# A reordered opening for a Fourier mixing and channel mix kernel: x on 96 partitions with one stride, mu turned by TensorE, small work on GpSimd

The kernel runs on one core of one Trainium2 chip. The metric is the device time of one execution in microseconds (us). Several executions are timed, and medians are quoted. The span in a profile, from the first to the last instruction, is 1.7 to 1.9 us shorter than the device time of the same execution, so spans and times can be compared by that difference.

## The reference

```python
def _attn_ref(x):                       # x: 8 x 3072 x 256
    X = np.fft.fft(x, axis=1)
    X = np.fft.fft(X, axis=2)
    return X.real.astype(np.float32)

def _moe_ref(x, mu_k, mu_r, w_k, w_v, w_r):
    x_prev = np.concatenate([zeros, x[:, :-1, :]], axis=1)
    xk = mu_k * x + (1.0 - mu_k) * x_prev
    xr = mu_r * x + (1.0 - mu_r) * x_prev
    k = np.maximum(xk @ w_k, 0.0)       # 256 x 1024
    v = k * k @ w_v                     # 1024 x 256
    r = 1.0 / (1.0 + np.exp(-(xr @ w_r)))
    return (r * v).astype(np.float32)
# the result is _moe_ref(_attn_ref(x), ...)
```

## The kernel before

Each batch goes through five stages. Stage A sums x over 48 rows with cosine and sine weights `w_pm`. Stage D does the transform over the 256 features with `w_eo`. Stage C does the rest of the transform over the rows with `m1` and `m2`. VectorE then forms `y`, its difference `d` to the previous row, and the mixes `x = y + mu * d`. The products follow: k pieces, a square, v tiles, and an r item with a sigmoid. The second half of the rows (`m = 1`) is the mirror image of the first, and for it the mixes need mu with its feature blocks swapped (`mu_m`). TensorE runs matmuls on zeros (`keep_busy`) where it would stand idle in the opening. From about 40 us on, it works without rest on the products of one batch and the transforms of the next.

```python
    def load_part(b, h, n, q0, nq):              # two loads of 48 partitions
        for g in range(2):
            r0 = 32 * g + 16 * h + q0
            nc.gpsimd.dma_start(out=xh_t[b, h][48 * g:48 * g + 48, q0:q0 + nq],
                                in_=x_r[b, :, r0:r0 + nq, :])

    def keep_busy(n):
        ps = ps_v()
        for _ in range(n):
            nc.tensor.matmul(out=ps[:, 0:512], lhsT=zeros[:, 0:P], rhs=zeros, ...)

    def gather(dst, w, n):                       # rows of w in the order of row_i
        nc.gpsimd.indirect_dma_start(dst, None, w,
                 bass.IndirectOffsetOnAxis(ap=row_i[:, n:n + 1], axis=0))

    def loads():
        V.memset(mu_f, 0.0)
        # ... mu: six small loads on the SP queue ...
        for a in range(2):
            gather(wk_sb[0][a], moe_w_k, a)
        for i, mu in enumerate(mus):
            gather(mu_f[:, 1, i:i + 1], mu, 1)
        load_xh(1, 0)
        for a in range(2):
            gather(wr_sb[0][a], moe_w_r, a)
        nc.gpsimd.dma_start(out=wv_sb, in_=moe_w_v.rearrange("(fc p) v -> p fc v", p=128))
        load_xh(1, 1)
        for a in range(2):
            gather(wk_sb[1][a], moe_w_k, 2 + a)
        for a in range(2):
            gather(wr_sb[1][a], moe_w_r, 2 + a)

    # ... stages A, D, C of batch 0; then each step of the k loop runs k_piece,
    # the "x" items due at it, a v_tile, and the "w" items due at it ...
    at(5, plain_128)                             # small tables, on VectorE
    at(7, mirrored_mu)                           # mu_m, on VectorE
```

## Time and profile before

| kernel before | value | from |
|---|---|---|
| median of 3 timed runs | 457.84 us (457.7 to 458.09) | the times |
| the profiled execution | 461.26 us, span 459.5 us | the same list, one line below |
| TensorE busy | 447.2 us, 97% | the page |
| ScalarE, VectorE busy | 358.8, 360.0 us, 78% each | the page |
| TensorE busy from 10 to 20, 20 to 30, 30 to 40 us | 7.45, 6.66, 9.26 us | busy time by stretch |
| first v tile | 35.75 us | TensorE's timeline |

The profile is of one execution, and this one took 3.4 us longer than the median.

"Time lost" by a moment is that moment less the matmul work that TensorE has begun by then, with fillers left out and each matmul priced at its start-to-start distance in a packed run (512 columns 214.5 ns, 256 columns 108.7 ns, and so on). The useful work of the whole program is 434.2 us in either kernel, so time lost can be compared between kernels with different orders.

### The profile page before, as it was taken

What the parts mean: (1) busy time and instruction counts of PE and PEld (TensorE: products, weight loads), DVE (VectorE), ACT (ScalarE), POOL (GpSimd) and SP (SyncE); (2) the same over time, 40 slices, a digit from 0 to 9 for tenths busy, and PEclk for the clock granted to TensorE, in tenths of its full rate; (3) what the DMA queues carried; (4) which work ended last, traced back from release to release, by engine and by line L of the source; (5) the groups of instructions that cost most, each with busy time, mean ns of one, the idle gap of its engine ahead of it and who ended that gap; (6) DMA issues with size and microseconds to landing.
All of it is one profiled execution on the core that took longest, in us unless ns stands there. A gap on an engine that the chain in (4) does not pass through costs nothing.

```text
span 459.5 us, 9804 instructions
## 1 busy us (share of the span) xinstructions
PE 447.2 (97%) x4087; PEld 327.6 (71%) x4087; DVE 360.0 (78%) x532; ACT 358.8 (78%) x398; POOL 35.6 (8%) x67
## 2 busy tenths in 40 slices
PE   8879999999999999999999999999999999999996
PEld 4647777777777777777777777777777777676764
DVE  7779988987788877978698777888679855898453
ACT  4689898888877887888887888878887888666661
POOL 8831000000000000000000000000000000000000
PEclk9999999999999999999999999999999999999999
DMA  7894561626622274214722265212222221223223
GB/s 131 128 177 90 120 140 46 124 64 138 124 62 67 49 146 109 70 48 90 164 68 58 59 136 120 69 48 69 55 63 61 56 70 47 71 64 75 70 68 93
DMA packets 32972, 40.25 MB, mean 88 GB/s; under 512 B 4480, under 2 KB 30592, under 8 KB 31584
## 3 DMA queue, kind: packets, MB, share of 16 engines
q1 hardware_dynamic: 28080, 25.07, 21.9%
q0 software_dynamic: 4688, 14.42, 18.8%
q8 instruction: 32, 0.52, 0.5%
q10 hardware_dynamic: 160, 0.13, 0.1%
q14 instruction: 12, 0.10, 0.1%
HBM read 28.84 MB, written 25.17 MB: 118 GB/s over the span
## 4 chain that ended last, share of the span: by engine, by line
PE 93%; ACT 3%; DMA 1%; POOL 1%; issue 1%; DVE 0%; another core or an unknown queue 0%; POOLq 0%
PE psV L592 36%; PE psW L555 35%; PE psW L578 9%; PE psW L431 5%; PE psW L407 4%; PE psW L458 3%; DMA xh<-in_x_dram 1%; ACT rl L565 1%; ACT g_all L395 1%; PE psW L421 1%; POOL xh L106 1%; ACT a L395 0%; ACT L583 0%; ACT pq L395 0%; ACT m L287 0%
## 5 line engine op out<-in xcount | busy, mean ns | idle before, releaser
L565 ACT ACTIVATE rl<-psW 128x1024 f16<-128x1024 f32 x192 | 196.7, 1026 | 80.8 <-PE psW L555 80.4
L555 PE MATMUL psW<-x,wk 128*128 128x512 f16 (+1 forms) x776 | 197.4, 377 | 2.5 <-ACT rl L565 1.5
L592 PE MATMUL psV<-wv_sb,k 128*128 128x256 f16 x1536 | 198.6, 272 | 0.0
L571 DVE TENSOR_TENSOR k<-rl 128x2048 f16<-128x2048 f16 x96 | 117.4, 1224 | 62.5 <-ACT rl L565 61.8
L592 PEld LDWEIGHTS <-k 128*128 128x128 f16 x1536 | 143.7, 98 | 20.3
L555 PEld LDWEIGHTS <-wk 128*128 128x128 f16 x776 | 75.7, 98 | 53.3 <-issue 4.0
L602 DVE SCALAR_TENSOR_TENSOR o<-psV,r 128x512 f32<-128x512 f32 (+1 forms) x97 | 66.3, 684 | 22.9 <-PE psV L592 20.7
L523 DVE TENSOR_TENSOR x<-y,t 128x1536 f16<-128x1536 f16 (+1 forms) x70 | 61.8, 882 | 2.4
L395 ACT ACTIVATE a<-psW 128x768 f16<-128x768 f32 x62 | 49.6, 806 | 4.0 <-PE psW L421 2.1
L578 PE MATMUL psW<-wr,x 128*128 128x256 f16 x384 | 49.8, 273 | 0.0
L583 ACT ACTIVATE r<-psW 128x1024 f16<-128x1024 f32 x48 | 49.0, 1021 | 0.8 <-PE psW L578 0.8
L578 PEld LDWEIGHTS <-x 128*128 128x128 f16 x384 | 37.6, 98 | 14.4 <-issue 0.2
L395 ACT ACTIVATE g_all<-psW 128x1024 f16<-128x1024 f32 (+1 forms) x46 | 46.9, 1022 | 1.1 <-PE psW L431 1.1
L106 POOL DMA_DIRECT2D xh<-in_x_dram x38 | 19.7, 525 | 238.7 <-DVE eo L119 222.7
L431 PEld LDWEIGHTS <-a 128*128 128x128 f16 x384 | 25.1, 98 | 10.0 <-issue 0.2
L407 PEld LDWEIGHTS <-eo 96*128 96x128 f16 x416 | 23.4, 97 | 11.6
L119 DVE TENSOR_TENSOR eo<-xh 96x2048 f16<-96x2048 f16 x26 | 31.5, 1213 | 0.0
L395 ACT ACTIVATE pq<-psW 128x896 f16<-128x896 f32 (+5 forms) x33 | 28.7, 871 | 1.6 <-PE psW L431 1.1
L431 PE MATMUL psW<-w_eo,a 128*128 128x128 f16 x368 | 27.7, 219 | 0.0
L407 PE MATMUL psW<-w_pm,eo 96*128 96x96 f16 x416 | 26.3, 205 | 0.0
L458 PEld LDWEIGHTS <-g_all 128*128 128x128 f16 x459 | 17.8, 98 | 7.7 <-issue 0.7
L510 DVE TENSOR_SCALAR t<-d,mu_f 128x1536 f16<-128x1536 f16 (+1 forms) x38 | 20.6, 543 | 0.1
(106 smaller groups left out, 158.5 us busy)
## 6 DMA issues: line engine op xcount, KB each, us to landing
out_dram<-o SPq DMA_DIRECT2D x190, 128.0 KB
xh<-in_x_dram POOLq DMA_DIRECT2D x28, 384.0 KB
xh<-in_x_dram POOLq DMA_DIRECT2D x6, 192.0 KB
wv_sb<-in_moe_w_v_dram POOLq DMA_DIRECT2D x1, 512.0 KB
xh<-in_x_dram POOLq DMA_DIRECT2D x4, 96.0 KB
out_dram<-o ACTq DMA_DIRECT2D x2, 64.0 KB
out_dram<-o SPq DMA_DIRECT2D x2, 64.0 KB
y<-f SPq DMA_DIRECT2D x7, 3.4 KB
```

Source lines behind the costliest of these rows:

```text
L395: nc.scalar.activation(out=out_ap, in_=in_ap, func=AF.Copy)
L407: nc.tensor.matmul(out=ps[:, 128 * i:128 * i + 96], lhsT=eo[:, 8 * j + i, e, :], rhs=w_pm[0:96, 0], start=True, stop=True)
L431: nc.tensor.matmul(out=_v(ps, 256 * i + 64 * (1 - e), [(128, 2), (1, 64)]), lhsT=a_t[b][:, e, 2 * u:2 * u + 2, :], rhs=w_eo[:, e, :], star ...
L458: nc.tensor.matmul(out=ps[:, o + 64 * i:o + 64 * i + 64], lhsT=g_all[:, u, col:col + 128], rhs=m[:, sl] if sl != 1 else mz[:, 0 if m is m1 ...
L523: V.tensor_tensor(out=dst, in0=_v(y_t[b], 64 * (NSL * a + lo + 3 * m), [(1, n)]), in1=_v(x_t["t", a], 64 * lo, [(1, n)]), op=ALU.subtract ...
L555: nc.tensor.matmul(out=st["k", ds][:, 512 * hs + lo:512 * hs + hi], lhsT=wk_sb[m][a][:, 128 * fc:128 * fc + 128], rhs=xk[:, a, 512 * i + l ...
L565: nc.scalar.activation(out=st["rl"][:, 2 * ds:2 * ds + 2], in_=st["k", ds].rearrange("p (f t) -> p f t", f=2), func=AF.Relu, bias=0.0, sca ...
L571: V.tensor_tensor(out=k2_t[c][:, 2 * ds - 2:2 * ds + 2], in0=r, in1=r, op=ALU.mult)
L578: nc.tensor.matmul(out=ps[:, 256 * tb:256 * tb + 256], lhsT=x_t[b, 1, m][:, a, 512 * i + 128 * tb: 512 * i + 128 * tb + 128], rhs=wr_sb[m] ...
L583: nc.scalar.activation(out=st["r", c], in_=ps, func=AF.Sigmoid)
L592: nc.tensor.matmul(out=st["v"][:, 256 * h:256 * h + 256], lhsT=k2_t[c][:, fc, 128 * tb:128 * tb + 128], rhs=wv_sb[:, fc], start=(fc == 0), ...
L602: V.scalar_tensor_tensor(out=o.rearrange("p a b -> p (a b)")[:, 0:256 * n], in0=st["v"][:, 0:256 * n], scalar=16.0, in1=st["r", c][:, 256 ...
```

## The change

The intent: end the opening sooner. x comes with one load of 96 partitions per part, since the row index is now split so that one stride serves all of them. mu comes as two plain rows and is turned to columns by four small matmuls, so two gathers and six small loads go. GpSimd computes the feature angles, and later `m_last`, `plain_128` and the mirror of mu. Stage A's evacuations (the copies of its results out of PSUM, where matmuls write) alternate between ScalarE and VectorE. The first k pieces come ahead of the rest of the long sine, stage D and stage C. The fillers fall from 22 matmuls to 17.

```diff
-    def load_part(b, h, n, q0, nq):
-        for g in range(2):
-            r0 = 32 * g + 16 * h + q0
-            nc.gpsimd.dma_start(out=xh_t[b, h][48 * g:48 * g + 48, q0:q0 + nq],
-                                in_=x_r[b, :, r0:r0 + nq, :])
+    def load_part(b, h, q0, nq):
+        nc.gpsimd.dma_start(out=xh_t[b, h][:, q0:q0 + nq],
+                            in_=x_r[b, :, 16 * h + q0:16 * h + q0 + nq, :])
@@
-    keep_busy(11)
+    keep_busy(10)
@@
+    def mu_turn():
+        ps = ps_v()
+        for a in range(2):
+            for i in range(2):
+                c = 2 * a + i
+                nc.tensor.matmul(out=ps[:, c:c + 1], lhsT=mu_p[:, a, i], rhs=one, ...)
+        V.tensor_copy(out=mu_f.rearrange("p a i -> p (a i)"), in_=ps[:, 0:4])
@@
+    def m_last():
+        ts = nc.gpsimd.tensor_scalar
+        for out, src, by in ((m2[hi64, 25], m1[hi64, 25], -1.0), ...):      # four
+            ts(out=out, in0=src, scalar1=by, scalar2=None, op0=ALU.mult)
+        for m in (m1, m2):
+            nc.gpsimd.memset(m[lo64, 25], 0.0)
@@ loads
-        for i, mu in enumerate(mus):
-            gather(mu_f[:, 1, i:i + 1], mu, 1)
@@ plain_128: V.tensor_copy, V.memset, V.tensor_scalar become
+        ts = nc.gpsimd.tensor_scalar
+        # ... four of 64x26, four of 64x1, one of 128x1, three memsets ...
@@
     def mirrored_mu():
         for a in range(2):
-            V.tensor_copy(out=mu_m[:, a], in_=mu_f[:, 1 - a])
-        V.tensor_copy(out=mu_m[0:1], in_=mu_f[0:1])
+            nc.gpsimd.tensor_copy(out=mu_m[:, a], in_=mu_f[:, 1 - a])
+        nc.gpsimd.tensor_copy(out=mu_m[0:1], in_=mu_f[0:1])
@@ the order of the opening and of the first steps
-    keep_busy(3)
+    keep_busy(1)
+    a_sum(0, 0, 8, "V")
@@
-    keep_busy(2)
-    a_sum(0, 1, 0)
-    a_sum(0, 1, 4, "V")
+    a_sum(0, 1, 0, "V")
+    a_sum(0, 1, 4)
+    mu_turn()
@@
+    at(1, m_sine, NS1, NSL)
+    at(2, m_last)
+    at(3, d_pair, 0, 16)
+    at(5, plain_128)
+    at(5, mirrored_mu)
     (many more items moved; cut)
```

## The prediction

> **What bounds the kernel now.** I read the page first, then the busy time by stretch, then the engines' timelines of the first 40 us. The page's line of busy time and its row of PE slices:
>
> ```profile
> PE 447.2 (97%) x4087; PEld 327.6 (71%) x4087; DVE 360.0 (78%) x532; ACT 358.8 (78%) x398; POOL 35.6 (8%) x67
> ...
> PE   8879999999999999999999999999999999999996
> ```
>
> TensorE (PE) is the bound everywhere but in the first three slices (11.5 us each) and the last. The stretches say how far that goes (columns: window, its length, then busy us of PE, weight loads, DVE, ACT, POOL, then clock, DMA share, GB/s written):
>
> ```profile
> 0.00:10.00 10.00, 8.71 (x47) 4.98 (x48) 7.84 (x41) 4.25 (x6) 8.40 (x27) 1.00 0.76 123
> 10.00:20.00 10.00, 7.45 (x99) 5.87 (x98) 7.57 (x25) 5.85 (x10) 8.31 (x10) 1.00 0.78 118
> 20.00:30.00 10.00, 6.66 (x71) 4.49 (x70) 7.44 (x23) 8.18 (x10) 6.65 (x8) 1.00 1.13 178
> 30.00:40.00 10.00, 9.26 (x95) 6.65 (x93) 9.65 (x27) 9.97 (x12) 0.59 (x2) 1.00 0.47 84
> 40.00:50.00 10.00, 10.00 (x94) 7.23 (x92) 9.79 (x20) 8.49 (x11) 1.51 (x3) 1.00 0.94 174
> ...
> 200.00:400.00 200.00, 200.00 (x1858) 147.42 (x1856) 154.84 (x197) 163.47 (x180) 4.03 (x8) 1.00 0.33 75
> ```
>
> From 40 us to the tail PE never rests, and its matmuls run at their stream rate (eight of 256 columns in 0.87 us, four of 512 in 0.86). The change leaves that work alone, so it can only win before 40 us. Where PE stood or ran filler there:
>
> ```profile
> 1.18 4.87 PE L142 MATMUL psV<-zeros 128*128 128x512 f16 x11 [1.18 <-DVE zeros L136]
> ...
> 11.80 2.14 PE L421 MATMUL psW<-w_pm,xh 96*128 96x192 f16 x24 [1.29 <-DMA xh<-in_x_dram]
> ...
> 15.22 0.59 PE L142 MATMUL psV<-zeros 128*128 128x512 f16 x2 [0.62 <-ACT a L395]
> ...
> 25.31 1.02 PE L555 MATMUL psW<-x,wk 128*128 128x512 f16 x4 [0.92 <-ACT rl L565]
> 26.23 0.61 PE L431 MATMUL psW<-w_eo,a 128*128 128x128 f16 x8
> 28.37 0.82 PE L421 MATMUL psW<-w_pm,xh 96*128 96x192 f16 x8 [1.53 <-issue]
> ...
> 37.43 1.02 PE L555 MATMUL psW<-x,wk 128*128 128x512 f16 x4 [0.64 <-ACT r L583]
> ```
>
> The useful work that PE had done by 37.43, counted from the code and priced at start-to-start distances in this trace: stage A sums of batch 0, 64 matmuls x 82 ns = 5.3; stage D, 48 x 56 ns = 2.7; stage C, 75 x 29 ns = 2.2; six k pieces x 0.86 = 5.2; one r item 0.9; one v tile 0.9; three stage A sums of batch 1 x 0.66 = 2.0. Sum 19.2 us. So 37.4 - 19.2 = **18.2 us lost in the opening**. About 6 of them end with the first useful matmul at 5.85 (start, weights w_pm, first x) and stay. At most some 12 us (2.6%) are there to win, and 2% would need 9.2 of them.
>
> The waits are of two kinds. Until 16 us it is x: 11.66 us passed before its second half was there. From 18 to 38 us it is ScalarE (ACT), which evacuates nearly everything, with three PSUM slots behind it. It also stood still twice with work queued:
>
> ```profile
> 20.29 1.03 ACT L395 ACTIVATE g_all<-psW 128x1024 f16<-128x1024 f32 x1 [0.92 <-PE psW L431]
> ...
> 27.29 1.02 ACT L395 ACTIVATE pq<-psW 128x1024 f16<-128x1024 f32 x1 [1.11 <-PE psW L431]
> ```
>
> The second drains stage C matmuls that by their records ended at 24.4 us; PE's semaphore came at 27.27. With 0.41 before the activation at 28.73 that is 2.4 us which I cannot explain; later in the run I found no such lag. It matters below.
>
> **What the Trainium skill says.** (1) "DMA: Bandwidth & Descriptors", Rules for kernel authors: two transfers to disjoint partition halves gain nothing over one, as both spread over the same 16 engines; its Specifications put the HBM limit of a core near 358 GB/s. The trace agrees: from 6 to 11 us 172, 193, 168, 166, 191 GB/s of fp16 were written, mean 178, read as fp32 at twice that, 356. So one load of 96 partitions in place of two of 48 saves issue time on GpSimd, not bytes. (2) "ScalarE: Activation LUTs", What ACT_TABLE_LOAD costs: an activation takes 186 ns + 0.833 ns per column, and neighbours overlap by 93 ns; the trace agrees (1026 ns for 1024 columns, 1039 by the formula). (3) "TensorE: Matmul & The Clock Gate", Part 1: a cold array runs at half rate for about 3.4 us; the first 11 fillers took 443 ns each against 213 later. One filler fewer at the front shouldn't move that. (4) "SBUF — State Buffer", Who interferes with whom: some VectorE (DVE) modes lock GpSimd out of its port. The trace before neither shows nor excludes it (small GpSimd tensor_scalars took 190 to 400 ns); moving angles to GpSimd invites it.
>
> **The change part by part.**
>
> *x loads.* Each part was two issues of some 0.5 us (the first pair 1.24 to 2.41); it becomes one. Five parts save about 2.5 us of GpSimd. But the stream is at the HBM limit from 4 us on, so x arrives earlier only by the fuller start (61 and 119 GB/s in the third and fourth us): about 0.6 us, 11.0 for 11.66.
>
> *Feature angles on GpSimd.* Two 128x128 and one 128x1 tensor_scalar, estimate 0.4 + 2 x 0.5 us, between the second and third x load. GpSimd has that time from the line above; the third load is still issued by about 5.2, before the first two have drained. VectorE loses 0.15 + 0.48 of work there, off the path.
>
> *Zeros of g_all.* Of VectorE's 0.65 + 0.14 us, to ScalarE: 11 x 128 columns, an estimate of 1.36 us by (2), plus two of 0.2. With the table load until 2.0 and three copies of mu it ends near 4.7, where the sine of w_pm is due (4.8 now). No cost, if the mu rows (two plain loads) have landed by 4.
>
> *mu.* Six tiny loads, two GpSimd gathers (14.11 to 16.77) go. Four small matmuls come, estimate 0.7 us of PE in front of the last stage A items. The gathers delayed batch 1 and the other weights. GpSimd should now end its issues near 23 instead of 27.87, and the loads land by about 31 instead of 34.5. Nobody on PE waits for them in the trace before.
>
> *Stage A evacuations.* From seven on ScalarE (0.81 each, 0.48 the half) and two on VectorE to an alternation (0.96 on VectorE). After x at 11.0: items end on PE at 11.7, 12.3, then mu 13.0, 13.7, 14.0, 14.4; VectorE has mu's copy, m_ends (1.0), eo_rest (0.34), then the last half-size item, 14.5 to 15.05. Stage D starts at 15.1 for 15.81: **0.7 us won**.
>
> *Stages D, C.* d_half copies 0.60 (ACT) and 0.69 (DVE) as before; the first C item 16.6 (16.88 now); ScalarE drains C, C, D, D by 20.3; the nine-to-seventeen C item now comes before k: PE 20.35 to 21.05, then the k halves to 22.8.
>
> *The start of the k loop.* This is the large part. The long second sine (1.24) shrinks to 10 slices (about 0.85), and the rest of stage D, stage C, the r item and batch 1's sums are put behind the first four k pieces. ScalarE: relu k0, k1 by 24.3, sine 25.1, k2 26.1, k3 27.1 (32.29 now). One square (1.23) later, 28.4, the first v tile can run (35.75 now). From there at one ScalarE instruction of 1.0 us after another: d_halves, k, D, k, C, k, sigmoid table 1.28 and r 1.02 by about 36, then two sums of batch 1. PE follows: k4 by 25.4, D item 26.4, an idle stretch of about 2 us for the square, v 29.3, and on with small waits, the largest on r near 36, to the end of the fourth v tile at **39.0 us**. By then it has done 5.3 + 2.7 + 2.2 + eight k pieces 6.9 + four v tiles 3.5 + r 0.9 + four sums 2.6 = 24.1 us. Lost: 39.0 - 24.1 = **14.9 us against 18.2: 3.3 won**. mu's matmuls are counted among the lost.
>
> *The rest* (plain_128, m_last, mu's mirror on GpSimd): about 2 us of VectorE work after 35 us, where PE is the bound: nothing.
>
> My schedule has ScalarE never stalled unexplained. Of the 2.4 us of now I let a third return, 0.8. **3.3 - 0.8 = 2.5 us: 457.84 becomes 455.3 us**, 0.5%.
>
> **The rivals.**
> (a) *ScalarE is the wall and hardly gets lighter.* It was 99.7% busy from 30 to 40 us; the evacuations moved off it are about 1.6 us of some 25, while zeros and mu rows come only while it idles. If the late lags return in full, or VectorE's chain (96% there) sets the pace instead, the gain is 0.5 to 1: 457. For it: VectorE gets 1 us more work in 11 to 15 us. Against it: what moves behind is work that the later slack (78% busy) absorbs.
> (b) *x sets everything.* If x still lands at 11.66, stage D starts at 15.7 and 0.6 is lost: 456.
> (c) *The lags belong to GpSimd's gathers*, since they came among them and never later; fewer and earlier gathers would clear them. Then 3.3 and a little more, as the reordered start has no 1.5 us hole: 453.5 to 454.5.
> (d) *GpSimd or mu late*: angles held up by VectorE's port, or the mu copies in front of w_pm's sine waiting for a load; each us there delays x or the first matmuls one for one: up to 459.
>
> **Range and chances.** The centre is 455.3. (a) and (b) make 456 to 457, (c) 453.5; runs agree within 0.1%. Eight in ten: 452.8 to 457.3. Over 2% faster is below 448.7, which needs three quarters of all that can be won at all: 0.03. Over 2% slower is above 467, a mishap such as PE cold for many us: 0.02.
>
> **What would show it.** Right: first x issue near 0.6 us on GpSimd and x's second half at about 11; stage D near 15.1; first v tile near 28.5; PE without waits from about 39; the stretch from 40 us on as now; ScalarE near full from 20 to 38. Wrong: stage D not before 15.6 (b); ScalarE idle behind finished matmuls for 2 us or more (a); none at all (c); an early wait of ScalarE on mu (d). A change of PE's busy time after 60 us would refute the first step, that only the opening can move.

## The result

The changed kernel took **458.61 us** in the median (457.98 to 459.18, 4 runs), the kernel before 457.92 us in the same rounds (457.7 to 458.09). The ratio is 1.0015, 95% interval 0.9998 to 1.0032. A ratio here and below is the mean time of one kernel's fast runs over that of the other's of the same rounds, so not quite the ratio of the medians quoted. The time was outside the range of 452.8 to 457.3 us, and the gain of 2.5 us did not come.

The page of the changed kernel, the same two lines as in the prediction:

```profile
PE 446.3 (98%) x4090; PEld 327.8 (72%) x4090; DVE 356.9 (78%) x497; ACT 360.6 (79%) x407; POOL 35.6 (8%) x71
...
PE   8989899999999999999999999999999999999995
```

Its busy time by stretch, with the columns named in the prediction:

```profile
10.00:20.00 10.00, 8.96 (x131) 7.40 (x129) 8.72 (x26) 6.87 (x11) 8.51 (x14) 1.00 0.92 131
20.00:30.00 10.00, 8.87 (x88) 5.99 (x86) 8.06 (x13) 9.57 (x12) 3.94 (x4) 1.00 1.08 208
30.00:40.00 10.00, 9.55 (x83) 7.01 (x81) 9.21 (x13) 9.03 (x12) 6.08 (x12) 1.00 0.28 54
40.00:50.00 10.00, 8.78 (x87) 6.50 (x85) 8.06 (x13) 7.55 (x10) 3.92 (x12) 1.00 0.64 123
...
200.00:400.00 200.00, 200.00 (x1856) 147.52 (x1853) 156.03 (x199) 163.19 (x179) 2.03 (x4) 1.00 0.33 75
```

TensorE gained work from 10 to 40 us, as planned. But from 40 to 50 us, where it had been busy for 10.00 of 10 us, it now shows 8.78. TensorE's timeline has the milestones and the new hole:

```profile
9.74 1.49 PE L441 MATMUL psW<-w_pm,xh 96*128 96x192 f16 x16 [0.28 <-DMA xh<-in_x_dram]
...
14.62 0.61 PE L451 MATMUL psV<-w_eo,a 128*128 128x128 f16 x8
...
26.46 0.60 PE L615 MATMUL psV<-wv_sb,k 128*128 128x256 f16 x4 [0.80 <-ACT g_all L415]
...
47.63 0.81 PE L578 MATMUL psW<-x,wk 128*128 128x512 f16 x3 [1.22 <-DVE x L547]
```

The first line is x's second half (11.80 before), the second stage D, the third the first v tile. In the kernel before, stage D and the first v tile stood at

```profile
15.65 0.61 PE L431 MATMUL psV<-w_eo,a 128*128 128x128 f16 x8
...
35.75 1.04 PE L592 MATMUL psV<-wv_sb,k 128*128 128x256 f16 x8
```

The last line of the changed kernel is a k piece that waits for the mixed x of the second half of the rows. Who kept VectorE from mixing it stands in VectorE's timeline of the changed kernel:

```profile
43.31 0.62 DVE L534 TENSOR_SCALAR t<-d,mu_m 128x1536 f16<-128x1536 f16 x1 [1.84 <-POOL mu_m L678]
```

and why GpSimd was late, in GpSimd's:

```profile
33.45 2.93 POOL L351 TENSOR_SCALAR m<-m 64x64 f16<-64x64 f16 x4 [8.60 <-DMA wr<-in_moe_w_r_dram,row_i]
...
38.15 3.23 POOL L400 TENSOR_SCALAR tw<-m 64x26 f16<-64x26 f16 x4
...
41.60 1.07 POOL L404 TENSOR_SCALAR tw<-tw 64x1 f16<-64x1 f16 x4
...
43.10 0.18 POOL L678 COPY mu_m<-mu_f 1x4 f32<-1x4 f32 x1
```

GpSimd had issued its last gather by 24.86 us. Then it stood for 8.60 us until the last gathered weights had landed, although its next four instructions (`m_last`) read no weights, and what they do read was there when VectorE's `m_swap` ended at 25.87 us. The program's own wait list for the first of them holds the semaphores of the late gathers, which came at 31.3, 32.6, 32.9 and 33.3 us. Why the compiler put them there I did not find out. After `m_last`, twelve small instructions of `plain_128` lie in front of the mirror copy.

Time lost in the two profiles, and in one of the experiments below (the kernel before with its late loads held back):

| time lost by | 15 us | 20 | 25 | 30 | 40 | 45 | 50 | 60 | 400 | span |
|---|---|---|---|---|---|---|---|---|---|---|
| before, first profile | 9.8 | 12.2 | 14.3 | 17.1 | 18.2 | 18.4 | 18.5 | 18.5 | 20.3 | 459.5 |
| changed, first profile | 9.4 | 11.3 | 11.7 | 13.1 | 13.9 | 13.9 | 15.2 | 15.4 | 17.0 | 456.6 |
| before_gated | 9.8 | 12.0 | 13.0 | 13.8 | 15.2 | 15.4 | 15.4 | 15.6 | 17.3 | 456.5 |

Two things stand out. The profiles differ by 4.3 us at 40 us and by 2.9 us in span, yet the timed runs differ by nothing. And the changed kernel hands back 1.3 us between 45 and 50 us. The first is a question of which execution the profile caught. The second is a wait that the change created.

### The profile page after: what moved, and what is told of

Same layout as the page of the kernel before. It is cut to its first block, busy times and chain, and to the rows that moved or that the text cites. A ratio compares the mean times of both kernels' runs of the same rounds, so it can differ in the third digit from the quotient of the medians.

```text
span 456.6 us, 9765 instructions
## 1 busy us (share of the span) xinstructions
PE 446.3 (98%) x4090; PEld 327.8 (72%) x4090; DVE 356.9 (78%) x497; ACT 360.6 (79%) x407; POOL 35.6 (8%) x71
## 4 chain that ended last, share of the span: by engine, by line
PE 89%; POOL 5%; DMA 2%; DVE 2%; issue 1%; POOLq 0%
PE psV L615 35%; PE psW L578 34%; PE psW L601 9%; PE psW L451 4%; PE psW L427 4%; PE psW L482 2%; DMA wr<-in_moe_w_r_dram,row_i 2%; POOL wk L359 1%; POOL wr L359 1%; POOL tw L400 1%; POOL m L351 1%; DVE x L547 0%; POOL row L290 0%; DVE t L534 0%; POOL w_eo L395 0%
## 5 line engine op out<-in xcount | busy, mean ns | idle before, releaser
L547 DVE TENSOR_TENSOR x<-y,t 128x1536 f16<-128x1536 f16 x60 | 57.5, 959 | 2.1
L601 PEld LDWEIGHTS <-x 128*128 128x128 f16 x384 | 37.6, 98 | 14.6 <-DVE k L594 0.4
L415 ACT ACTIVATE pq<-psW 128x896 f16<-128x896 f32 (+5 forms) x33 | 28.5, 868 | 0.9 <-PE psW L482 0.9
L104 POOL DMA_DIRECT2D xh<-in_x_dram x19 | 10.2, 540 | 225.6 <-DVE eo L117 224.5
L482 PEld LDWEIGHTS <-g_all 128*128 128x128 f16 x459 | 17.8, 98 | 7.9 <-ACT g_all L415 1.1
L534 DVE TENSOR_SCALAR t<-d,mu_m 128x1536 f16<-128x1536 f16 x32 | 19.7, 615 | 1.8 <-POOL mu_m L678 1.8
```

Of the source, the lines that this page charges most:

```text
L415: nc.scalar.activation(out=out_ap, in_=in_ap, func=AF.Copy)
L547: V.tensor_tensor(out=dst, in0=_v(y_t[b], 64 * (NSL * a + lo + 3 * m), [(1, n)]), in1=_v(x_t["t", a], 64 * lo, [(1, n)]), op=ALU.subtract ...
L601: nc.tensor.matmul(out=ps[:, 256 * tb:256 * tb + 256], lhsT=x_t[b, 1, m][:, a, 512 * i + 128 * tb: 512 * i + 128 * tb + 128], rhs=wr_sb[m] ...
```

## The experiments

The questions were: is the profile of the kernel before typical of it; what does the wait for mu's mirror cost; and what are the late TensorE semaphores, seen as ScalarE standing idle behind matmuls that have long ended? A semaphore is the counter by which one engine tells another that a result is ready. "Late" below means that TensorE's semaphore came more than 0.12 us behind the end of its matmul. They were looked for on all engines, and only TensorE's were found late. But in the nine profiles that have late ones, 6 to 20 updates of the semaphores of TensorE, VectorE and ScalarE left no record at all, and in the other eleven at most one. So the others' may have been late unseen, and whether the recording itself takes part in the lateness was not tested. The kernels of one call ran on one chip and share the runs of the kernel before.

### First call: both kernels again, and GpSimd's small work back on VectorE

*before_again*: no edit, the kernel before.

> The kernel before, unchanged, profiled a second time. Theory P (untypical profile): the profiled execution from which I predicted took 461.26 us, 3.4 us more than the 457.84 of the unprofiled ones, and the excess is the three late PE semaphores in its opening; a second profile has a span near 456.1 us, no semaphore of PE more than 0.2 us behind its matmul, and only some 14.8 us lost in the opening. Rival R (the profile was right): the span is again near 459.5 us with the same lags at 18.7 to 21 and 24.4 to 28.8 us, so the opening has 18.2 us lost in every run. Ratio of the timed runs 1.000 under both.

Measured: 458.91 us against 459.69 (11 runs, 458.57 to 461.87) of the same kernel beside it, ratio 0.9977 (0.9942 to 1.0013). That two sets of runs of one kernel differ by 0.23% on one chip is the yardstick for all ratios below. The span was 457.4, and 16.2 us were lost by 40 us, not 18.2. There were late semaphores again, between 17.1 and 28.3 us, by up to 1.9 us instead of 2.9. So neither theory held as it stood: the kernel before need not lose 18.2 us, but its late semaphores were no single accident.

*after_again*: no edit, the changed kernel.

> The changed kernel, unchanged, timed in more rounds and profiled again. Both theories: ratio 1.000 to 1.003 as on record, span 456.2 to 457.4 us, TensorE waiting 1.2 us near 46.4 us for VectorE's mix, which waits for GpSimd's mirror of mu. If the profile of this kernel shows that wait in one execution only, it isn't the place where the gain went.

Measured: 459.92 us, ratio 0.9997 (0.9962 to 1.0032), with two slow runs of six (466.99 and 466.94 us at a mean clock of 0.98 and 0.985). The profile lost 16.4 us by 40 us. Here the changed kernel has late semaphores too (17.1 to 25.0 us), and with TensorE behind, the wait for the mirror costs only 0.2 us between 45 and 50.

*after_mu_v*: the mirror on VectorE.

```diff
         for a in range(2):
-            nc.gpsimd.tensor_copy(out=mu_m[:, a], in_=mu_f[:, 1 - a])
-        nc.gpsimd.tensor_copy(out=mu_m[0:1], in_=mu_f[0:1])
+            V.tensor_copy(out=mu_m[:, a], in_=mu_f[:, 1 - a])
+        V.tensor_copy(out=mu_m[0:1], in_=mu_f[0:1])
```

> The changed kernel with the mirror of mu (three tiny copies) back on VectorE; all else on GpSimd as changed. Theory G (GpSimd's chain of small operations gives back part of the opening's gain): TensorE's 1.2 us wait near 46 us goes, VectorE pays 0.4 us off the path, time 1.0 to 1.3 us less than the changed kernel, ratio to before 0.998 to 0.999. Rival (that wait is covered by later slack or by the next bound): same as the changed kernel within 0.3 us.

Measured: 461.27 us, ratio 1.0016 (0.9978 to 1.0053), two slow runs of six. The wait itself was gone (17.8 us lost at 45, 17.7 at 50), but the profile shows 17.6 lost by 40 us: late semaphores at 23.9 and 25.4 us, and a clock that was cut to half from 15.3 to 18.7 us. The run could not tell what the wait is worth. The mend was timed again in the fifth call.

*after_small_v*: `m_last`, `plain_128` and the mirror all on VectorE (`nc.gpsimd` becomes `V` in the three).

```diff
     def m_last():
-        ts = nc.gpsimd.tensor_scalar
+        ts = V.tensor_scalar
@@ plain_128
-        ts = nc.gpsimd.tensor_scalar
-        nc.gpsimd.memset(w_eo[:, 0, 63:64], 1.0)
+        ts = V.tensor_scalar
+        V.memset(w_eo[:, 0, 63:64], 1.0)
     (the other memsets and the mirror likewise)
```

> The changed kernel with all its small late GpSimd operations (last fixes of m, plain_128, mirror of mu) back on VectorE. Theory G: no better than moving the mirror alone, since only the mirror is on the path; VectorE has about 2.2 us more work near 26 and 37 us, where it is 92% busy, so 0 to 1 us slower than with the mirror alone moved: ratio to before 0.998 to 1.001. Rival (GpSimd's operations hold up VectorE's through the shared port as well): faster than the mirror alone by 0.5 us or more.

Measured: 461.87 us, ratio 1.0039 (1.0007 to 1.0071), one slow run of six. Late semaphores again, and a new loss of 1.4 us from 50 to 60 us, where VectorE is now behind. To move all of the small work back is too much.

### Second call: late loads held back, gathers removed, the mirror early

*before_gated*: in the kernel before, x's last part for batch 1 and the four late gathers wait for a relu of the k loop, by a one-element copy on GpSimd that reads its result.

```diff
-        load_xh(1, 1)
-        for a in range(2):
-            gather(wk_sb[1][a], moe_w_k, 2 + a)
-        for a in range(2):
-            gather(wr_sb[1][a], moe_w_r, 2 + a)
+    gate_t = const.tile([1, 2], FP16)
+    def late_loads(part):
+        nc.gpsimd.tensor_copy(out=gate_t[0:1, part:part + 1], in_=st["rl"][0:1, 0, 0:1])
+        if part == 0:
+            load_xh(1, 1)
+        else:
+            (the four gathers)
@@
+    at(0, late_loads, 0)
+    at(4, late_loads, 1)
```

> The kernel before, with batch 1's second x load held back until the first relu (25 us) and the second halves of w_k and w_r until the fifth (some 33 us), each by a one-element GpSimd copy that waits for it. What I want to know is why TensorE's semaphores come up to 2.9 us late in the opening of the profiles so far (at 16 to 21 and 20 to 29 us), and never later. Theory D (the saturated DMA queues delay them): with less in flight after 24 us the late ones at 24 to 29 us are gone or shrink below 0.5 us, and the fast runs gather at 456 to 457.5 us, 1 us or more below the kernel before. Rival I (the indirect loads and the small packets of w_v at 22 to 27 us): late ones as before, same time.

Measured: 458.29 us against 458.72, ratio 1.0004 (0.9982 to 1.0025); one run of the kernel before took 949.95 us and is left out. No late semaphore, 15.2 us lost by 40 us, span 456.5. ScalarE's timeline of before_again, in which an evacuation waits behind TensorE:

```profile
25.43 1.02 ACT L395 ACTIVATE pq<-psW 128x1024 f16<-128x1024 f32 x1 [0.98 <-PE psW L431]
```

and the same evacuation in before_gated, with no wait:

```profile
24.11 1.03 ACT L402 ACTIVATE pq<-psW 128x1024 f16<-128x1024 f32 x1
```

It is the instruction that waited 1.11 us and started at 27.29 in the first profile of the kernel before. Between these three executions of practically one instruction stream it starts at 24.11, 25.43 and 27.29.

*before_nogather*: plain strided loads in place of all gathers, and no row numbers computed for them on GpSimd (`rows()` goes). The rows come in a wrong order, so the result is wrong.

```diff
     def gather(dst, w, n):
-        nc.gpsimd.indirect_dma_start(dst, None, w,
-                                     bass.IndirectOffsetOnAxis(ap=row_i[:, n:n + 1], axis=0))
+        # row 0 or 128, then 64 and 63 rows with a step of 2
+        nc.gpsimd.dma_start(out=dst[0:1], in_=w[first:first + 1])
+        for p0, m, k in ((1, 64, 1), (65, 63, 2)):
+            ...
+            nc.gpsimd.dma_start(out=dst[p0:p0 + m], in_=src)
```

> The kernel before with each indirect load in place of which stand three plain strided loads of the same bytes; the upper halves come in ascending order, so the result is wrong on purpose. Theory D: late semaphores of TensorE as before, time the same within 1 us. Rival I (indirect loads): none late by more than 0.2 us, 1 to 3 us faster.

Measured: 458.68 us, ratio 1.0014 (0.9991 to 1.0038), no late semaphore, 14.9 us lost by 40 us. So the gathers cost nothing else that TensorE feels. But the next kernel shows that this chip had no late semaphores even with gathers, so the run does not settle who makes them.

*after_fix*: the mirror is copied by VectorE right behind mu's columns, and four fillers come back.

```diff
         V.tensor_copy(out=mu_f.rearrange("p a i -> p (a i)"), in_=ps[:, 0:4])
+        for a in range(2):
+            V.tensor_copy(out=mu_m[:, a], in_=mu_f[:, 1 - a])
+        V.tensor_copy(out=mu_m[0:1], in_=mu_f[0:1])
@@
-    keep_busy(1)
+    keep_busy(3)
@@
     mu_turn()
+    keep_busy(2)
@@
-    at(5, mirrored_mu)
```

> The changed kernel with the mirror of mu made by VectorE right after mu is turned (0.5 us at 12.5 us) and four more fillers (two before the third stage A item, two after mu is turned). Theory G with cold clock: the wait at 46 us is gone in every execution, and the fillers keep the array's clock from being cut between 9 and 19 us, so no run is slow (2 of 6 were, at clocks of 0.98) and the fast ones lie at 456.5 to 458.5 us, about 1 us below the changed kernel beside it on the same chip (459.6 to 460.0). Rival (opening limited by late semaphores): fast runs as the changed kernel's within 0.5 us.

Measured: 458.07 us against 458.72, ratio 0.9998 (0.9973 to 1.0024). No late semaphores with all gathers in place. Lost: 14.8 us at 40, 15.0 at 45 and at 50. The mirror's wait is gone, but the copies and fillers ahead of stage D cost about as much: the changed kernel's first profile had lost 13.9 by 40.

*after_fix_gated*: after_fix with the late loads held back as in before_gated.

```diff
+    at(0, late_loads, 0)
+    at(4, late_loads, 1)
```

> The same with the late loads held back as in the first of these runs. Theory D: no late semaphore, fast runs 455 to 457 us, the best of all. Rival I: like after_fix within 0.5 us, with late semaphores at 20 to 25 us.

Measured: 457.82 us (457.68 to 458.17), ratio 0.9991 (0.997 to 1.0011). 14.6 us lost by 40 us, no late semaphores: within noise of after_fix.

### Third call: a chip with late semaphores

*before_third*: no edit, the kernel before.

> The kernel before once more, profiled on whatever chip comes. Its span has ranged from 456.0 to 460.1 us so far. If TensorE's semaphores come late in its profile, span 457 to 460 us with more than 16 us lost by 50 us; if none does, about 456.3 us with 15.2 lost. This is the yardstick for the gated one beside it.

Measured: 459.29 us against 460.23 (11 runs, 459.24 to 462.83) of itself, ratio 0.9985 (0.9962 to 1.0008). Late semaphores at 16.3 to 17.1 and 25.5 to 28.6 us; 16.5 us lost by 40.

*before_gated2*: before_gated again.

```diff
+    at(0, late_loads, 0)
+    at(4, late_loads, 1)
```

> The kernel before with the late loads held back, on the same chip as the one above. Theory D (saturated DMA queues delay TensorE's semaphores): none late here even where the one above shows them, and the median of the timed runs at least 0.8 us lower if those show a spread of 2 us or more. Rival (the lateness comes with the chip or the execution, not with these loads): late ones here as often as above, medians within 0.5 us.

Measured: 458.58 us, ratio 0.9967 (0.9944 to 0.9989). The late semaphores between 20 and 30 us were gone, two at 16.2 and 17.1 us stayed, and three new ones came at 35.9 to 37.5 us. In this profile the held-back gathers were issued from 31.09 to 36.98 us. So in this profile they followed the gathers, and not the fullness of the queues: from 20 to 30 us, with x's held-back part under way, the DMA engines were as busy as in before_third (a share of 1.10 for 1.09), and no semaphore was late. 14.7 us lost by 40.

*after_third*: no edit, the changed kernel.

> The changed kernel, third profile. With semaphores in time: 13.9 us lost by 45 us, 15.2 by 50, span 456.3 to 456.8. With late ones: 16.4 or more lost by 45 us, no wait at 46 us. Either way the mirror of mu on GpSimd is ready no sooner than 43 us, as it waits for the last weight load to land near 33.4 us.

Measured: 460.11 us, ratio 0.9999 (0.9976 to 1.0021). 16.8 us lost by 40. TensorE's stage C matmuls in this profile,

```profile
20.75 0.52 PE L482 MATMUL psW<-m,g_all 128*128 128x64 f16 x12 [0.39 <-ACT g_all L415]
```

ended at 21.27 us by their records. ScalarE's evacuation of them:

```profile
23.07 1.02 ACT L415 ACTIVATE pq<-psW 128x1024 f16<-128x1024 f32 x1 [2.37 <-PE psW L578]
```

In the first profile of the changed kernel this evacuation began 0.04 us behind its matmuls, at 20.05 against 20.01. Here it is 1.8 us. Nothing in the program differs between the two.

*after_muv_gated*: the changed kernel with the mirror on VectorE at its old place and the late loads held back.

```diff
-            nc.gpsimd.tensor_copy(out=mu_m[:, a], in_=mu_f[:, 1 - a])
-        nc.gpsimd.tensor_copy(out=mu_m[0:1], in_=mu_f[0:1])
+            V.tensor_copy(out=mu_m[:, a], in_=mu_f[:, 1 - a])
+        V.tensor_copy(out=mu_m[0:1], in_=mu_f[0:1])
@@
+    at(0, late_loads, 0)
+    at(4, late_loads, 1)
```

> The changed kernel with the mirror on VectorE at its old place and the late loads held back, without extra fillers. Theory G: no wait on the mirror, so with semaphores in time some 14.0 us lost by 50 us for 15.2, span 455.3 to 455.8 us, 0.5 to 1.3 us below both kernels: ratio to before 0.997 to 0.999. Rival (the fillers were needed): the array's clock is cut between 9 and 19 us in a third of the runs, which then take 466 us.

Measured: 458.43 us (457.86 to 458.61) against 460.23, ratio 0.9957 (0.9935 to 0.9978), the lowest of all. 15.1 us lost by 40, and 15.4 by 50. Three semaphores were late here too, at 17.8 to 18.0 us, just behind the issue of the first four gathers (to 17.3 us).

### Fourth call: which of the held-back loads it is

*gate_gathers_only*: the kernel before, with only the four gathers held back.

```diff
         load_xh(1, 1)
-        (the four gathers)
+    def late_loads(part):
+        (the one-element copy, then the four gathers)
@@
+    at(4, late_loads, 1)
```

> The kernel before with only the four indirect loads of the second halves of w_k and w_r held back to some 31 us; batch 1's second x load comes early as before, so the DMA queues stay as full until 30 us. Theory I2 (an indirect load at work delays TensorE's semaphores): none late at 20 to 29 us, perhaps some at 31 to 38; as fast as with both held back, 0.6 to 1.2 us below the kernel before on a chip whose runs of it spread by 2 us. Theory D2 (the fullness of the queues does): late ones at 20 to 29 us as before.

Measured: 457.7 us against 457.88 (11 runs), ratio 0.9991 (0.9974 to 1.0007), no late semaphore, 14.2 us lost by 40.

*gate_x_only*: only x's last part held back, behind the gathers.

```diff
-        load_xh(1, 1)
@@
+    def late_x():
+        nc.gpsimd.tensor_copy(out=gate_t[0:1, 0:1], in_=st["rl"][0:1, 0, 0:1])
+        load_xh(1, 1)
@@
+    at(0, late_x)
```

> The reverse: the four indirect loads early as before, batch 1's second x load held back to some 24 us. Theory I2: late ones at 20 to 29 us as in the kernel before, time as before within 0.4 us. Theory D2: none late, 0.6 us or more faster.

Measured: 461.87 us, ratio 1.0093 (1.007 to 1.0116). No late semaphore either, so this pair does not tell gathers from x: this chip showed none with gathers left alone. What cost 0.9% is a plain wait. The waits of the profile (who waited for whom: us in total, times, the longest):

```profile
DVE eo L119 <- DMA xh<-in_x_dram: 3.6, 1, 3.6
...
PE psW L583 <- DVE x L528: 3.0, 2, 2.6
```

x came 3.6 us too late for VectorE's first butterfly, and everything in VectorE's fixed order behind it, the r item's mixes among them, came later. Behind the gathers, x is not held back for nothing.

*nogather_again*: before_nogather again.

```diff
-        nc.gpsimd.indirect_dma_start(dst, None, w, ...)
+        (three plain loads)
```

> The kernel before with plain strided loads instead of all indirect ones (result wrong on purpose), once more on another chip. Theory I2: none late by more than 0.2 us again, 0.6 us or more below the kernel before where that spreads by 2 us. Theory D2: some late at 20 to 29 us.

Measured: 458.61 us, ratio 1.001 (0.999 to 1.0029), no late semaphore, 15.5 us lost by 40.

*after_muv_gated2*: after_muv_gated again.

```diff
+            V.tensor_copy(out=mu_m[:, a], in_=mu_f[:, 1 - a])
@@
+    at(0, late_loads, 0)
+    at(4, late_loads, 1)
```

> The best version so far again, on another chip: span 456 to 457 us, spread under 1 us, ratio to before 0.995 to 0.999.

Measured: 457.08 us (456.78 to 458.8) against 457.88, ratio 0.9985 (0.9966 to 1.0003). Its busy time by stretch, to be held against the changed kernel's:

```profile
30.00:40.00 10.00, 9.50 (x83) 6.96 (x82) 9.26 (x16) 8.98 (x12) 8.11 (x11) 1.00 0.57 93
40.00:50.00 10.00, 10.00 (x100) 7.56 (x98) 9.83 (x15) 8.58 (x10) 5.79 (x8) 1.00 0.50 94
```

The hole of 40 to 50 us is closed: 10.00 us busy for 8.78. 13.8 us were lost by 40 and 13.9 by 50.

### Fifth call: the mirror alone

*after_fourth*: no edit, the changed kernel.

> The changed kernel once more, beside its own one-line mend, so that the two are timed on one chip. Theory M (the wait for mu's mirror on GpSimd costs TensorE about 1.3 us between 45 and 50 us in an execution without late TensorE semaphores): 0 to 0.4 us over the kernel before, ratio 1.000 to 1.001, and the profile shows VectorE waiting 0.4 to 1.9 us for the mirror. Rival N (the wait is only seen because TensorE ran ahead, and is paid back elsewhere): the same here; the two differ in the next run.

Measured: 459.29 us against 457.99 (11 runs, 457.06 to 459.02), ratio 1.0029 (1.0003 to 1.0055). The profile shows no late semaphore, but lost 15.8 us by 40. Its row of the granted clock on the page, in tenths of full speed for 40 slices, has an 8 in the second slice. The busy time by stretch says how much: a mean of 0.83 from 10 to 20 us (third column from the end).

```profile
PEclk9899999999999999999999999999999999999999
```

```profile
10.00:20.00 10.00, 8.89 (x103) 7.75 (x103) 7.36 (x21) 5.45 (x10) 8.51 (x14) 0.83 0.91 137
```

In its clock record, full speed was granted at 4.7 us, taken back at 15.0 and given again at 18.4. VectorE then waited for the mirror, but less than in the first profile, since the others were late as well:

```profile
44.04 0.62 DVE L534 TENSOR_SCALAR t<-d,mu_m 128x1536 f16<-128x1536 f16 x1 [0.44 <-POOL mu_m L678]
```

*after_mu_v2*: after_mu_v again, the mirror alone on VectorE.

```diff
-            nc.gpsimd.tensor_copy(out=mu_m[:, a], in_=mu_f[:, 1 - a])
-        nc.gpsimd.tensor_copy(out=mu_m[0:1], in_=mu_f[0:1])
+            V.tensor_copy(out=mu_m[:, a], in_=mu_f[:, 1 - a])
+        V.tensor_copy(out=mu_m[0:1], in_=mu_f[0:1])
```

> The three mirror copies on VectorE, nothing else. Theory M: 0.7 to 1.5 us under the changed kernel of the same call where that one shows the wait for the mirror and no late semaphores, ratio to the kernel before 0.9975 to 0.9990, and time lost does not grow between 45 and 50 us. If late semaphores show (as on the two chips before where they did), the mirror is ready in time anyhow and the gain is under 0.5. Rival N: within 0.4 us of the changed kernel even without late semaphores.

Measured: 457.28 us, ratio 0.9984 (0.9968 to 1.0001). The difference of 2.0 us to after_fourth is two things mixed, and the list of the executions with the mean clock of each takes them apart:

| span, us | clock 0.998 or more | clock 0.994 or less |
|---|---|---|
| after_fourth | 456.3, 456.6 | 457.4, 457.5, 457.6, 460.4 |
| after_mu_v2 | 455.1, 455.1, 455.1, 455.8 | 457.0, 457.1 |
| the kernel before beside them | 455.3 to 457.2, mean 456.3 (all 11 at 0.997 or more) | none |

Down the column without a cut, the mirror's wait is worth 456.45 - 455.3 = **1.2 us**, by two executions against four. With a cut it is worth 457.5 - 457.05 = 0.45 us (460.4 left out), which agrees with the wait of 0.44 us above. The rival, that the wait is paid back elsewhere, had allowed 0.4 us. The traces are against it too: the changed kernel's first profile has lost 1.3 us more than after_muv_gated2 at 50 us, and still 1.3 us more at 400. Across a row, a cut of the clock costs 1.1 us in after_fourth and 1.8 us in after_mu_v2. By their mean clock four executions of six had a cut in after_fourth and two of six in after_mu_v2 (where it fell is known only for the two profiled ones), which makes up the rest of the 2.0 us.

## Why the prediction was wrong

**The step that failed: "18.2 us lost in the opening".** The count was right for the execution that was profiled. Its execution took 461.26 us, and the gain worked out from it was taken off a median of 457.84. In executions of the kernel before without late TensorE semaphores 14.2 to 15.5 us were lost by 40 us (before_gated, before_nogather, gate_gathers_only, gate_x_only, nogather_again, each with its small edit). The timed runs on the first chip have no trace, but their time tells as much: the span less the time lost by 60 us is 440.7 to 441.2 us in all 20 profiles, so what makes executions differ lies before 60 us, and a span of 457.84 - 1.75 = 456.1 us means some 15.2 us lost by then, where the profiled execution had lost 18.5. The forecast of **14.9 us for the changed kernel** was near: 13.9 measured. Taken from some 15.0, it says a gain of 0.1 us; with the 13.9 measured, 1.1 us. The forecast said 3.3.

**"Of the 2.4 us of now I let a third return, 0.8".** This is where the mistake enters the sum. The unexplained stalls were named, measured, and then treated as a property of the kernel before that the change would largely remove. They are a property of the execution and the chip: on the first chip the kernel before had them in its profile and the changed one did not; on two later chips all six profiles without held-back loads had them (before_again, before_third, after_again, after_third, after_mu_v, after_small_v), and the two with held-back loads had some; on the other two chips none of the ten profiles had, though the kernel before was not profiled there without an edit. Rival (a), "if the late lags return in full", came nearest to what happened on the first two, but still gave a gain of 0.5 to 1 us, where the ratios are 0.9997 and 0.9999. Rival (c) put the lags down to the gathers, which the traces bear out (see "Left open"), but that fewer gathers would clear them did not hold: the changed kernel has two fewer and lost 16.4 and 16.8 us there.

**"plain_128, m_last, mu's mirror on GpSimd: nothing".** Wrong, and this is the new wait. The working looked at VectorE's saving and not at who waits for GpSimd's result. mu's mirror, formerly three copies on VectorE, stood at the end of GpSimd's queue behind a landing at 33.3 us and 18 small instructions, and was ready at 43.3. It cost 1.3 us of TensorE in the first profile, and 1.2 us by the times of the fifth call. "PE without waits from about 39" was wrong for this reason.

**"But the stream is at the HBM limit from 4 us on, so x arrives earlier only by the fuller start", about 0.6 us.** Mis-sized, to the good: x's second half was at work 2.1 us earlier (9.74 for 11.80). What the prediction took for a limit, 178 GB/s written or 356 read, was none: from 4 to 10 us the changed kernel wrote 206 GB/s for 174 before, which is 412 read, and the kernel before itself wrote 213 and 221 GB/s in the two us from 20 on. Which part of the change brought it, the one load for two or the small loads that went, was not separated.

**"One filler fewer at the front shouldn't move that."** True of the first warm-up, and too narrow. The change takes five fillers of 22. "TensorE: Matmul & The Clock Gate" of the Trainium skill, Part 1, What's actually happening, says that the clock is granted by how busy the array has been in windows of about 3.4 us. The traces agree with the length: where the clock was cut in the opening, it was 3.4 us at half speed, each time 10.2 us behind the first grant, in after_mu_v, after_fourth and after_mu_v2. In these three TensorE was busy for 7.6, 7.6 and 7.75 us of the 10.2 us between grant and cut; in the other 17 profiles for 7.8 or more in as long a time, a narrow margin. That fewer fillers are the reason is argued from this, not shown. The counts of executions do not settle it, and a mean clock does not tell where a cut fell: 0.996 or less came in 6 of 60 of the kernel before, 7 of 22 of the changed one, 7 of 12 with the mirror alone on VectorE (after_mu_v and after_mu_v2), and 1 of 8 with four fillers put back (after_fix and after_fix_gated). But it also came in only 1 of 12 of after_muv_gated, which has no extra fillers, and in 3 of 6 of gate_x_only, which has all 22.

**Right.** Only the opening moved: from 60 to 400 us the first two profiles lose 1.8 and 1.6 us, and TensorE is busy for 200.00 of 200 us in both. The first x issue took 0.66 us (near 0.6 expected). GpSimd's issues ended at 24.86 us (near 23 expected, 27.87 before). x's second half was worked on from 9.74 us (11.0 expected, 11.80 before), stage D from 14.62 (15.1), the fourth relu ended at 25.92 (27.1), and the first v tile ran from 26.46 (28.5). Rivals (b) and (d) fell with these. The schedule of the opening was, if anything, too cautious.

**The sum as measured**, for executions without late semaphores and cuts, in the fifth call: the opening wins 1.0 us (455.3 against 456.3, the mirror on VectorE), the mirror on GpSimd takes 1.2 back, and the changed kernel stands at 456.45 (two executions): level with the kernel before. The cuts of the clock then bring it above on that chip.

**Left open.** How a semaphore comes late, and why on some chips or at some moments only. Where it happens the traces do tell, though the pair of runs meant for it could not. 162 updates of the semaphores of TensorE, VectorE and ScalarE have no record within 0.12 us of their instruction's end, in ten profiles together. All of them fall between the issue of the first indirect load of a group and 1 us behind the issue of its last one. In before_gated2 and after_muv_gated, whose gathers come in two groups, none falls into the 10.8 and 14.0 us between the groups, while plain loads run. So they go with gathers, and not with full queues. Gathers alone do not bring them: eight other profiles with gathers have none. Open too: why the program makes `m_last` wait for the gathers, and what sets off the slow runs of 466 us and more in the first call, five in 18 of changed kernels and none in 15 of the kernel before.

## What to carry to other kernels

Before a loss is read from a profile, hold the time of the profiled execution against the timed runs. If they differ by as much as the gain that is hoped for, subtract within executions of one kind, or profile again. When small work is moved to an idle engine, follow each result to its reader, and give the result that a critical reader needs its own place in the queue: three copies of at most 4 columns cost 1.2 us here because they stood behind others. The version with the mirror on VectorE, with or without the late loads held back, is the best of these kernels by most of its runs (ratios 1.0016 and 0.9984 without, 0.9957 and 0.9985 with), though only on one chip is it clear of the 0.15 to 0.23% by which the kernel before differs from itself.

## What the Trainium skill lacked or had wrong

- "SBUF — State Buffer", Who interferes with whom, says that the port pair which VectorE and GpSimd share is an exclusive lock, and that who starts second blocks until the first ends. It has no price for small GpSimd instructions, and the runs show one. Four 64x1 tensor_scalars on GpSimd took 1.07 us in the changed kernel's first profile, where VectorE stood idle from 41.46 us on. In after_third, where VectorE ran tensor_tensors of 2048 columns meanwhile, they took 2.85 us:

```profile
41.45 2.85 POOL L404 TENSOR_SCALAR tw<-tw 64x1 f16<-64x1 f16 x4
```

  So each was 0.22 us beside an idle VectorE and 0.66 us in the mean (0.21 to 1.18) beside a busy one. On VectorE itself (gate_x_only) the four took 0.65 us.
- "TensorE: Matmul & The Clock Gate", Part 1, What's actually happening, has the clock fall after an idle window of about 3.4 us; further down, Part 1 tells of a kernel whose many short pauses were enough, without a measure of them. In three profiles here it was cut for 3.4 us although TensorE was never idle for more than 0.9 us at a time and was busy for 7.6 to 7.8 us of the 10.2 us before.
- No page has TensorE semaphores that come late: up to 2.9 us behind the end of the matmul in the first profile of the kernel before, 1.9 us in before_again, none in eleven of the 20 profiles of nearly the same program. None says that records of semaphores go missing with them (6 to 20 in the nine profiles that have late ones).
- "Perfetto Trace Analysis" does not warn that the execution in the profile may be an unusual one: 461.26 us here against timed runs of 457.7 to 458.09.
